# Wk second in each load queue, in a fixed order, a shorter GpSimd chain per z2 tile, 48 warm-up products and a longer order search in a fused attention and gMLP kernel

## The chip, the cores and the metric

The kernel runs on one core of one Trainium2 chip, in one launch. The metric is the device time of that core in microseconds (us). An execution's time is its span in the trace, from the first to the last instruction, plus about 1.75 us. Each execution also records the mean granted clock of TensorE, 1.0 being full speed. Most executions have 0.998 or more, which I call *undisturbed*; some have about 0.993 and are some 2 us longer. The result lists call both kinds "fast" as long as they are within 1.5% of the kernel's fastest run, so the ratios can contain both. Where it matters I also give the undisturbed runs alone. Engine names in the profile: PE is TensorE, PEld its weight load, DVE VectorE, ACT ScalarE, POOL GpSimd, SP SyncE (it issues DMA).

## The reference

Two residual blocks over x of 2048 tokens by 512 (bf16):

```python
x = A_x
h  = x + A(layernorm(x), wqkv, wo)            # linear attention, 32 heads of 16
h2 = h + B(layernorm(h), w_in, w_sp, b_sp, w_out)

# A: q, k, v = split(x @ wqkv); pq, pk = phi(q), phi(k)
#    phi(t) = where(t > 0, t + 1, exp(t)) + 1e-6
#    kv = sum over s of pk v;  z = sum over s of pk;  o = (pq kv) / (pq z + 1e-6);  o @ wo
# B: z = gelu(x @ w_in)               # 2048 x 1792
#    z1, z2 = halves of z;  z2 = layernorm(z2)
#    g = w_sp @ z2 + b_sp             # w_sp is 2048 x 2048, it mixes tokens
#    (z1 * g) @ w_out
```

So there is one barrier: no product with w_sp can finish before the last of the 16 normalized z2 tiles (128 tokens each) is there.

Names in the profile: xn and hn are the normalized x and h, xnT and hnT their transposes; pk is phi(k), pqT is phi(q) transposed, e an exponential on the way to them; st and rs hold statistics and 1/sqrt(variance + epsilon); ident is the identity matrix with which TensorE transposes.

## The kernel before

The kernel records its operations in a list with their data dependences, then a search looks for an order of them with a cost model on the host, and the order that it finds is emitted as five static instruction streams with semaphores. The search is random but seeded, so a source always gives the same streams; any edit of a cost or of an operation gives others.

```python
LOOK = 100.0
ROUNDS = 400
# ... in schedule():
        best = self._swing([-o.prio for o in ops], 20)
        rng = np.random.default_rng(0)
        for _ in range(ROUNDS):
            # ... perturb the starts of a stretch of operations, schedule again
            if got[0] <= best[0]:
                best = got
        self.est, self.start = best
        self.seq = sorted(ops, key=lambda o: (self.start[o.i], o.i))
```

The head: loads, statistics and normalization of x on VectorE and GpSimd, transposes on TensorE, then the wk product:

```python
    load_x("SP", 0, 1, 2000)
    load_x("ACT", 1, 1, 2200)
    load_x("SP", 2, 1, 2700)
    load_x("ACT", 3, 1, 2900)
    for eng, c in (("SP", 0), ("ACT", 2)):
        dma(eng, wqkv[:, c:c + 2, D:2 * D], wq[:, c:c + 2, D:2 * D], f"wk{c}", issue=500, lat=3600, bias=prio())
    load_x("SP", 4, 2, 4600)
    load_x("ACT", 6, 2, 4800)
    # ... x8 to x14, wq
    def rstd(s, r, n, w, col, neg):
        rr, ss = r[:, n:n + w, :], s[:, n:n + w, :]
        pool(lambda p: p.tensor_scalar(rr[:, :, 1:2], ss[:, :, col + 1:col + 2], EPS_LN, None, op0=ALU.add),
             [ss[:, :, col + 1:col + 2]], [rr], 167)
        pool(lambda p: p.tensor_tensor(rr[:, :, 0:1], rr[:, :, 1:2],
                                       expo[:, 0:w].rearrange("p (a b) -> p a b", b=1), ALU.pow), [rr, expo], [rr], 535)
    # ...
    warmup(56)
```

The built order of the loads was x0, x4, x2, wk0, x8 and so on in SP's queue and x1, x3, wk2, x6 in ACT's. A z2 tile takes its moments either from VectorE (the odd tiles and tile 14) or, for the seven other even ones, from the sums that ScalarE accumulates; then GpSimd does six tiny steps:

```python
        if n % 2 == 0 and n < NT - 2:
            gl = act(z2[:, n, :], src, ACT.Gelu_apprx_tanh, FH, accum=s[:, 0:1])
            act(sq_t, z2[:, n, :], ACT.Square, FH, accum=s[:, 1:2])
            pool(lambda p, s=s: p.tensor_scalar(s[:, 12:13], s[:, 0:1], 1.0 / FH, None, op0=ALU.mult), [s], [s], 167)
            pool(lambda p, s=s: p.tensor_scalar(s[:, 1:2], s[:, 1:2], 1.0 / FH, None, op0=ALU.mult), [s], [s], 167)
            pool(lambda p, s=s: p.tensor_tensor(s[:, 2:3], s[:, 12:13], s[:, 12:13], ALU.mult), [s], [s], 167)
            pool(lambda p, s=s: p.tensor_tensor(s[:, 13:14], s[:, 1:2], s[:, 2:3], ALU.subtract), [s], [s], 167)
        else:
            # ... gelu, then bn_stats and bn_aggr on VectorE
        gl.deps.add(table.i)
        rstd(st3, rs3, n, 1, 12, False)
        norm("DVE", z2[:, n, :], z2[:, n, :], st3, rs3, n, 12, FH)
```

Of the kernel before, what the change touches and what calls it, by code (L numbers as in the profile page):

```python
# [6 lines left out]
ACT = mybir.ActivationFunctionType  # L7
ALU = mybir.AluOpType

P = 128  # L10
GRAN = 16
SEM_NS = 45.0
LOOK = 100.0
ROUNDS = 400


class _Op:
    __slots__ = ("i", "eng", "fn", "deps", "cost", "lat", "dma", "prio", "bias", "users",
                 "signal", "count", "clock", "sem", "tag")

    def __init__(self, i, eng, fn, cost, lat, dma, bias):
        self.i, self.eng, self.fn, self.cost, self.lat, self.dma, self.bias = i, eng, fn, cost, lat, dma, bias
        self.deps = set()
        self.users = []
        self.signal = False
        self.count = 0
        self.clock = None
        self.sem = None


class _Prog:
# [93 lines left out]
        return op  # L125

    def _lag(self, p, u):
        return p.lat + (0.0 if p.eng == u.eng == "PE" and p.dma is None else SEM_NS)

    def _pass(self, rank, back):  # L130

        ops = self.ops
        pre = [o.users if back else o.deps for o in ops]
        nxt = [o.deps if back else o.users for o in ops]
        left = [len(p) for p in pre]
        ready = [0.0] * len(ops)
        free = {e: 0.0 for e in self.ENGS}
        cand = {e: [] for e in self.ENGS}
        for o in ops:
            if not left[o.i]:  # L140
                cand[o.eng].append(o.i)
        start = [0.0] * len(ops)
        for _ in ops:
            best = None
            for e in self.ENGS:
                c = cand[e]
                if not c:
                    continue
                t0 = max(free[e], min(ready[i] for i in c))
                pick = min((i for i in c if ready[i] <= t0 + LOOK), key=lambda i: (rank[i], i))  # L150
                t0 = max(t0, ready[pick])
                if best is None or t0 < best[0]:
                    best = (t0, e, pick)
            t0, e, i = best
            cand[e].remove(i)
            start[i] = t0
            free[e] = t0 + ops[i].cost
            for u in nxt[i]:
                lag = self._lag(ops[u], ops[i]) if back else self._lag(ops[i], ops[u])
                ready[u] = max(ready[u], free[e] + lag)  # L160
                left[u] -= 1
                if not left[u]:
                    cand[ops[u].eng].append(u)
        return start
# [23 lines left out]
    def schedule(self):  # L188
        ops = self.ops
        for o in ops:  # L190
            for d in o.deps:
                ops[d].users.append(o.i)
        for o in reversed(ops):
            o.prio = max((ops[u].prio + self._lag(o, ops[u]) for u in o.users), default=o.lat) + o.cost + o.bias
# [3 lines that stand above are left out]
            t = np.array(best[1])  # L198
            a, w = rng.uniform(0, 0.6 * best[0]), rng.uniform(5e3, 4e4)
            if rng.random() < 0.4:  # L200
                a, w = 0.0, best[0]
            near = (t >= a) & (t < a + w)
            got = self._swing(list(t + near * rng.normal(0, rng.choice([200, 600, 1500, 3000]), len(ops))), 2)
# [4 lines that stand above are left out]
        self.order = {e: [o for o in self.seq if o.eng == e] for e in self.ENGS}  # L208
# [91 lines left out]
def bass_sequential_preLN__linear_attn_block__mixer_gmlp__prompt_kernel(  # L300
# [160 lines left out]
    def dma(eng, out_ap, in_ap, name, issue=100.0, lat=2500.0, **k):  # L461
        return g.add(eng, lambda q: q.dma_start(out_ap, in_ap), [in_ap], [out_ap], cost=issue, lat=lat, dma=name, **k)
# [19 lines left out]
                                   base=DH, channel_multiplier=-1), [bmask], [bmask], 350, bias=1e5)  # L482


    later = [1e6]

    def prio():
        later[0] -= 1e3
        return later[0]

    wq = A_wqkv.rearrange("(c p) f -> p c f", p=P)

    def load_w(eng, j, nm, lat):
        dma(eng, wqkv[:, :, j * D:(j + 1) * D], wq[:, :, j * D:(j + 1) * D], nm, issue=500, lat=lat, bias=prio())

    def load_x(eng, n, w, lat):
        dma(eng, x[:, n:n + w, :], x_d[n * P:(n + w) * P, :].rearrange("(n p) d -> p n d", p=P), f"x{n}", issue=500,
            lat=lat, bias=prio())

    def load(eng, dst, src, nm, lat, **k):  # L500
        return dma(eng, dst, src.rearrange("(c p) f -> p c f", p=P), nm, lat=lat, **k)

    load_x("SP", 0, 1, 2000)
    load_x("ACT", 1, 1, 2200)
    load_x("SP", 2, 1, 2700)
    load_x("ACT", 3, 1, 2900)
    for eng, c in (("SP", 0), ("ACT", 2)):
        dma(eng, wqkv[:, c:c + 2, D:2 * D], wq[:, c:c + 2, D:2 * D], f"wk{c}", issue=500, lat=3600, bias=prio())
    load_x("SP", 4, 2, 4600)
    load_x("ACT", 6, 2, 4800)  # L510
    for n, t in ((8, 5100), (10, 5600), (12, 6100), (14, 6700)):
        load_x("SP", n, 2, t)
    load_w("SP", 0, "wq", 7500)
    preload = g.add("ACT", lambda ac: ac.preload_act_table_set("natural_log_exp_and_others"), [], [], cost=1300)


    def stats(src, k, n):
# [1 line left out]
        dve(lambda v: v.bn_stats(s[:, 0:6], src[:, n, :]), [src[:, n, :]], [s[:, 0:6]], D)  # L519
        dve(lambda v: v.bn_aggr(s[:, 6:8], s[:, 0:6]), [s[:, 0:6]], [s[:, 6:8]], 14)  # L520

    def rstd(s, r, n, w, col, neg):

        rr, ss = r[:, n:n + w, :], s[:, n:n + w, :]
        pool(lambda p: p.tensor_scalar(rr[:, :, 1:2], ss[:, :, col + 1:col + 2], EPS_LN, None, op0=ALU.add),  # L525
             [ss[:, :, col + 1:col + 2]], [rr], 167)
        pool(lambda p: p.tensor_tensor(rr[:, :, 0:1], rr[:, :, 1:2],  # L527
                                       expo[:, 0:w].rearrange("p (a b) -> p a b", b=1), ALU.pow), [rr, expo], [rr], 535)
        if neg:
            for i in range(n, n + w):  # L530
                pool(lambda p, i=i: p.tensor_scalar(r[:, i, 2:3], s[:, i, col:col + 1], r[:, i, 0:1], -1.0,
                                                    op0=ALU.mult, op1=ALU.mult), [r[:, i, :], s[:, i, :]], [r[:, i, :]], 167)

    def norm(eng, dst, src, s, r, n, col, w):
        mean, rst, nmr = s[:, n, col:col + 1], r[:, n, 0:1], r[:, n, 2:3]
# [36 lines left out]
            return inst  # L572
        PE(fn, [warm], [bank(7, P)], 2200 + n * 54, bias=1e6)

    warmup(56)

    PAIRS = [0, 2]
    pc = [0]
# [149 lines left out]
    for n in range(NT):  # L728
        b = next_pair()

        def fn(pe, n=n, b=b):
            inst = None
            for c in range(KD):
                pe.matmul(bank(b), lhsT=hnT[:, c, n * P:(n + 1) * P], rhs=win[:, c, FH:FH + GW],  # L734
                          start=c == 0, stop=c == KD - 1)
            for c in range(KD):
                inst = pe.matmul(bank(b + 1, F2), lhsT=hnT[:, c, n * P:(n + 1) * P], rhs=win[:, c, FH + GW:F],  # L737
                                 start=c == 0, stop=c == KD - 1)
            return inst
        PE(fn, [hnT[:, :, n * P:(n + 1) * P], win[:, :, FH:F]], [bank(b), bank(b + 1)], KD * (216 + 162.5))  # L740
        src = pair(b).rearrange("p a b -> p (a b)")[:, 0:FH]
        s = st3[:, n, :]
        if n % 2 == 0 and n < NT - 2:
            gl = act(z2[:, n, :], src, ACT.Gelu_apprx_tanh, FH, accum=s[:, 0:1])
            act(sq_t, z2[:, n, :], ACT.Square, FH, accum=s[:, 1:2])
            pool(lambda p, s=s: p.tensor_scalar(s[:, 12:13], s[:, 0:1], 1.0 / FH, None, op0=ALU.mult), [s], [s], 167)
            pool(lambda p, s=s: p.tensor_scalar(s[:, 1:2], s[:, 1:2], 1.0 / FH, None, op0=ALU.mult), [s], [s], 167)
            pool(lambda p, s=s: p.tensor_tensor(s[:, 2:3], s[:, 12:13], s[:, 12:13], ALU.mult), [s], [s], 167)
            pool(lambda p, s=s: p.tensor_tensor(s[:, 13:14], s[:, 1:2], s[:, 2:3], ALU.subtract), [s], [s], 167)
        else:  # L750
            gl = act(z2[:, n, :], src, ACT.Gelu_apprx_tanh, FH)
            dve(lambda v, n=n, s=s: v.bn_stats(s[:, 0:6], z2[:, n, 0:GW]), [z2[:, n, 0:GW]], [s[:, 0:6]], GW)  # L752
            dve(lambda v, n=n, s=s: v.bn_stats(s[:, 6:12], z2[:, n, GW:FH]), [z2[:, n, GW:FH]], [s[:, 6:12]], F2)
            dve(lambda v, s=s: v.bn_aggr(s[:, 12:14], s[:, 0:12]), [s[:, 0:12]], [s[:, 12:14]], 14)
        gl.deps.add(table.i)
        rstd(st3, rs3, n, 1, 12, False)
        norm("DVE", z2[:, n, :], z2[:, n, :], st3, rs3, n, 12, FH)

    dma("SP", bsp, B_b_sp.partition_broadcast(P), "bsp", issue=1500, lat=2500).deps.add(g.last.i)
# [3 lines left out]
    k = 0  # L763
# [68 lines left out]
```

## Time and profile before

| what | before |
|---|---|
| time | 250.01 us, median of 3 (249.61 to 250.08) |
| span of the profiled run | 248.0 us, clock 1.000 |
| TensorE busy | 240.6 us, of which 56 warm-up products 5.58 |
| TensorE idle after 240 us | 3.10 us |

The page's first part gives the busy time of each engine, its share of the span, and its instructions:

```profile
PE 240.6 (97%) x1196; PEld 111.9 (45%) x1196; DVE 133.1 (54%) x270; ACT 86.2 (35%) x122; POOL 44.6 (18%) x134
```

TensorE is the limit: only its idle time, or time spent on warm-up, can be won. Where it idles shows in the windows view of before. Its columns are the stretch in us, its length, the busy time of PE, PEld, DVE, ACT and POOL with instruction counts, the granted clock, the DMA share and GB/s:

```profile
0.00:10.00 10.00, 7.72 (x77) 6.82 (x78) 6.19 (x17) 2.73 (x4) 4.66 (x22) 1.00 0.82 257
10.00:20.00 10.00, 10.00 (x53) 4.39 (x50) 9.73 (x26) 8.31 (x14) 5.05 (x13) 1.00 0.38 99
20.00:30.00 10.00, 9.55 (x45) 4.33 (x45) 6.84 (x12) 7.29 (x10) 3.02 (x8) 1.00 0.46 92
50.00:70.00 20.00, 19.75 (x91) 8.16 (x90) 19.51 (x34) 18.43 (x20) 2.38 (x6) 1.00 0.49 100
...
95.00:120.00 25.00, 23.70 (x116) 10.68 (x115) 13.73 (x31) 14.54 (x25) 12.75 (x38) 1.00 0.54 115
```

The stretches 30 to 50, 70 to 95 and 120 to 240 us are full. The list of TensorE's waits in before (total us, times, longest) names who ended each gap:

```profile
PE psum L432 <- ACT xnT L451: 0.9, 1, 0.9
PE psum L432 <- DVE z L537: 0.8, 1, 0.8
PE psum L734 <- DMA hnT<-hn: 0.5, 1, 0.5
PE psum L432 <- DVE pk L564: 0.5, 1, 0.5
```

The first is the gap before the first wk product, in the head; here is TensorE's timeline of before there (start us, us, what, and in brackets the idle time before it and what ended it):

```profile
1.22 5.58 PE L571 MATMUL psum<-warm 128*128 128x128 bf16 x56 [1.22 <-POOL warm L469]
6.93 0.72 PE L551 MATMUL psum<-ident,xn 128*128 128x128 bf16 x8
8.58 1.02 PE L432 MATMUL psum<-wqkv,xnT 128*128 128x512 bf16 x4 [0.93 <-ACT xnT L451]
```

The second is the gap of 0.84 us before the first w_sp product at 113.41. The chain of work that ended last shows what led to it. In the stretch from 89 to 114 us of before (start us, us, what) it runs on GpSimd for nearly all the time from 91.8 us on:

```profile
105.64 0.51 POOL st L746
106.22 0.22 POOL st L747
106.51 0.20 POOL st L748
106.78 0.20 POOL st L749
107.06 0.22 POOL rs L525
107.36 0.58 POOL rs L527
107.96 0.51 DVE z L537
```

The six POOL lines from 105.64 on are one even z2 tile: the scaling of two sums, a square, a subtraction, then the addition of epsilon and the power of -1/2. GpSimd's groups of instructions in before, by form (output and input shapes, count, busy us and mean ns, idle before):

```profile
L527 POOL TENSOR_TENSOR rs<-rs,expo 128x1 f32<-128x1 f32 x34 | 20.0, 600 | 1.3
L525 POOL TENSOR_SCALAR rs<-st 128x1 f32<-128x1 f32 x34 | 7.7, 234 | 53.3 <-DVE st L520 49.6 <-DVE st L754 2.9
L746 POOL TENSOR_SCALAR st<-st 128x1 f32<-128x1 f32 x7 | 2.0, 288 | 3.2 <-ACT sq L451 2.7
L749 POOL TENSOR_TENSOR st<-st 128x1 f32<-128x1 f32 x7 | 1.6, 227 | 0.5
L747 POOL TENSOR_SCALAR st<-st 128x1 f32<-128x1 f32 x7 | 1.5, 218 | 0.3
L748 POOL TENSOR_TENSOR st<-st 128x1 f32<-128x1 f32 x7 | 1.5, 209 | 0.5
```

One number in each of 128 partitions costs 0.2 to 0.3 us here, and the power 0.6 us.

### The profile page before, as it was taken

How to read it: one execution, taken by the hardware profiler on the slowest of the kernel's cores; microseconds unless marked ns; L12 is line 12 of the kernel's file. 1: busy time of each engine (PE TensorE's matmuls, PEld its weight loads, DVE VectorE, ACT ScalarE, POOL GpSimd, SP SyncE). 2: the span in 40 equal slices, each digit the busy share in tenths (PEclk: the TensorE clock that was granted, in tenths of full speed). 3: DMA queues.
4: the chain of work that ended last, by engine and by line, in shares of the span. 5: the costliest groups of instructions: out<-in, count | busy, mean ns of one | idle time of the engine just before them, and what ended most of it. 6: DMA issues, size and time to landing. Idle time of an engine off the chain costs nothing.

```text
span 248.0 us, 3139 instructions
## 1 busy us (share of the span) xinstructions
PE 240.6 (97%) x1196; PEld 111.9 (45%) x1196; DVE 133.1 (54%) x270; ACT 86.2 (35%) x122; POOL 44.6 (18%) x134
## 2 busy tenths in 40 slices
PE   8899999999999999998999999999999999999994
PEld 8443444534444454543444444444444444444441
DVE  3998565689999998482233322332123201443064
ACT  2588533699985679861000000000021000010020
POOL 5356000001125889751000000000000000000000
PEclk9999999999999999999999999999999999999999
DMA  6925396444544555554444542000000000102022
GB/s 194 313 46 107 83 382 218 102 105 90 94 100 102 106 87 100 151 115 85 106 101 96 89 100 62 0 0 3 0 0 0 3 0 0 63 24 74 11 71 99
DMA packets 57198, 21.57 MB, mean 87 GB/s; under 512 B 49504, under 2 KB 56544, under 8 KB 57184
## 3 DMA queue, kind: packets, MB, share of 16 engines
q1 hardware_dynamic: 56352, 20.59, 34.0%
q10 hardware_dynamic: 832, 0.79, 1.0%
q8 instruction: 9, 0.15, 0.2%
q14 instruction: 5, 0.04, 0.1%
HBM read 7.47 MB, written 2.10 MB: 39 GB/s over the span
## 4 chain that ended last, share of the span: by engine, by line
PE 65%; DVE 18%; POOL 8%; ACT 4%; issue 2%; DMA 2%; SPq 0%; POOLq 0%
PE psum L432 60%; POOL rs L527 5%; DVE st L519 5%; PE psum L613 4%; DVE h L715 4%; POOL rs L525 2%; ACT r L451 2%; DMA x<-in_A_x_dram 2%; DVE pqT L704 1%; DVE pk L564 1%; ACT e L451 1%; DVE z L537 1%; DVE pqT L564 1%; DVE hn L537 1%; DVE st L752 1%
## 5 line engine op out<-in xcount | busy, mean ns | idle before, releaser
L432 PE MATMUL psum<-wsp,z 128*128 128x512 bf16 x448 | 97.7, 379 | 0.8 <-DVE z L537 0.8
L432 PEld LDWEIGHTS psum<-wsp,z 128*128 128x128 bf16 x448 | 43.7, 98 | 54.0 <-DVE z L537 1.3
L451 ACT ACTIVATE z1T<-psum 128x512 bf16<-128x512 f32 x28 | 16.6, 596 | 121.4 <-PE psum L432 121.4
L795 DVE TENSOR_TENSOR u<-psum,bsp 128x512 bf16<-128x512 f32 x28 | 19.4, 691 | 53.6 <-PE psum L432 53.4
L797 DVE TENSOR_TENSOR z1T<-u,z1T 128x512 bf16<-128x512 bf16 x28 | 11.9, 424 | 29.1 <-ACT z1T L451 28.6
L432 PE MATMUL psum<-hnT,win 128*128 128x512 bf16 x112 | 26.5, 379 | 0.0
L432 PE MATMUL psum<-wout,z1T 128*128 128x512 bf16 x112 | 25.7, 379 | 0.0
L527 POOL TENSOR_TENSOR rs<-rs,expo 128x1 f32<-128x1 f32 (+1 forms) x41 | 25.1, 621 | 1.8
L451 ACT ACTIVATE e<-psum 128x1024 bf16<-128x1024 f32 (+1 forms) x18 | 16.6, 923 | 12.8 <-PE psum L432 12.3
L525 POOL TENSOR_SCALAR rs<-st 128x1 f32<-128x1 f32 (+1 forms) x41 | 9.3, 233 | 60.5 <-DVE st L520 56.7
L451 ACT ACTIVATE z<-psum 128x896 bf16<-128x896 f32 x16 | 14.6, 914 | 7.5 <-PE psum L737 7.2
L432 PE MATMUL psum<-wqkv,xnT 128*128 128x512 bf16 x64 | 15.7, 379 | 1.4 <-ACT xnT L451 0.9
L432 PEld LDWEIGHTS psum<-wout,z1T 128*128 128x128 bf16 x112 | 10.9, 98 | 13.4 <-DVE ost L785 0.6
L734 PE MATMUL psum<-win,hnT 128*128 128x512 bf16 x64 | 16.4, 379 | 0.5 <-DMA hnT<-hn 0.5
L613 PE MATMUL psum<-pk,xn 128*128 128x512 bf16 x64 | 16.4, 379 | 0.0
L432 PEld LDWEIGHTS psum<-hnT,win 128*128 128x128 bf16 x112 | 10.2, 98 | 13.4 <-ACT z1T L451 2.8
L432 PE MATMUL psum<-xnT,wqkv 128*128 128x512 bf16 x64 | 15.8, 379 | 0.3 <-DVE pqT L564 0.3
L432 PE MATMUL psum<-m,pqT 128*128 128x512 bf16 x64 | 15.7, 380 | 0.0
L785 DVE TENSOR_TENSOR ost<-psum,h 128x512 bf16<-128x512 f32 x16 | 10.4, 686 | 8.7 <-PE psum L432 8.6
L737 PE MATMUL psum<-win,hnT 128*128 128x384 bf16 x64 | 13.0, 326 | 0.0
L519 DVE BATCH_NORM_STATS2 st<-x 128x6 f32<-128x512 bf16 x16 | 10.4, 677 | 3.8 <-DMA x<-in_A_x_dram 3.8
L563 DVE TENSOR_SCALAR e<-e 128x1024 bf16<-128x1024 bf16 (+1 forms) x18 | 7.1, 394 | 9.4 <-ACT e L451 9.2
(67 smaller groups left out, 204.8 us busy)
## 6 DMA issues: line engine op xcount, KB each, us to landing
out_dram<-ost SPq DMA_DIRECT2D x16, 128.0 KB, 1.7
win<-in_B_w_in_dram SPq DMA_DIRECT2D x1, 1792.0 KB, 8.2
x<-in_A_x_dram SPq DMA_DIRECT2D x5, 256.0 KB, 7.0
wqkv<-in_A_wqkv_dram SPq DMA_DIRECT2D x2, 512.0 KB, 8.7
wsp<-in_B_w_sp_dram SPq DMA_TRANSPOSE x64, 2.9
wout<-in_B_w_out_dram SPq DMA_DIRECT2D x1, 896.0 KB, 11.1
wo<-in_A_wo_dram SPq DMA_DIRECT2D x1, 512.0 KB, 3.4
bsp<-in_B_b_sp_dram SPq DMA_DIRECT2D x1, 512.0 KB, 4.4
```

The source lines that it names most:

```text
L432: inst = pe.matmul(out_ap, lhsT=a, rhs=b, start=start and i == 0, stop=stop and i == len(pairs) - 1)
L451: return g.add("ACT", lambda ac: ac.activation(out_ap, in_ap, func, **kw), [in_ap, *extra], [out_ap] + ([accum] if accum is not None else []),
L519: dve(lambda v: v.bn_stats(s[:, 0:6], src[:, n, :]), [src[:, n, :]], [s[:, 0:6]], D)
L525: pool(lambda p: p.tensor_scalar(rr[:, :, 1:2], ss[:, :, col + 1:col + 2], EPS_LN, None, op0=ALU.add), [ss[:, :, col + 1:col + 2]], [rr], 167)
L527: pool(lambda p: p.tensor_tensor(rr[:, :, 0:1], rr[:, :, 1:2], expo[:, 0:w].rearrange("p (a b) -> p a b", b=1), ALU.pow), [rr, expo], [rr] ...
L613: inst = pe.matmul(bank(CB[c]), lhsT=xn[:, i, c * P:(c + 1) * P], rhs=pk[:, i, :], start=i == 0, stop=i == NT - 1)
L715: dve(lambda v, n=n, b=b: v.tensor_tensor(h[:, n, :], bank(b), x[:, n, :], ALU.add), [bank(b), x[:, n, :]], [h[:, n, :]], D, ps=True)
L734: pe.matmul(bank(b), lhsT=hnT[:, c, n * P:(n + 1) * P], rhs=win[:, c, FH:FH + GW], start=c == 0, stop=c == KD - 1)
L737: inst = pe.matmul(bank(b + 1, F2), lhsT=hnT[:, c, n * P:(n + 1) * P], rhs=win[:, c, FH + GW:F], start=c == 0, stop=c == KD - 1)
L785: dve(lambda v: v.tensor_tensor(o, bank(b), h[:, n, :], ALU.add), [bank(b), h[:, n, :]], [o], D, ps=True)
L795: dve(lambda v, t=t, b=b, tok=tok: v.tensor_tensor(t, bank(b), bsp[:, tok], ALU.add), [bank(b), bsp[:, tok]], [t], GW, ps=True)
L797: dve(lambda v, t=t, z=z: v.tensor_tensor(z, t, z, ALU.mult), [t, z], [z], GW, acc=2)
```

## The change

It does four things at once. It fixes the order of the loads in each queue (through "soft" predecessors that order the issue without a wait) with wk second and gives the search's cost model later landing times and longer GpSimd steps; the aim is an earlier first wk product. It takes three GpSimd steps out of an even z2 tile: ScalarE's Square gets a scale, so that its sum is the mean of squares, VectorE forms mean² minus that (the negative variance), and the addition of epsilon multiplies by -1. It lets the search look further (160 instead of 100) and longer (1200 rounds instead of 400). It takes 8 warm-up products away.

```diff
-LOOK = 100.0
-ROUNDS = 400
+LOOK = 160.0
+ROUNDS = 1200
# ... soft predecessors in the search, cut
-    load_x("SP", 0, 1, 2000)
-    load_x("ACT", 1, 1, 2200)
-    load_x("SP", 2, 1, 2700)
-    load_x("ACT", 3, 1, 2900)
+    load_x("SP", 0, 1, 2650)
+    load_x("ACT", 1, 1, 2850)
     for eng, c in (("SP", 0), ("ACT", 2)):
-        dma(eng, wqkv[:, c:c + 2, D:2 * D], wq[:, c:c + 2, D:2 * D], f"wk{c}", issue=500, lat=3600, bias=prio())
-    load_x("SP", 4, 2, 4600)
-    load_x("ACT", 6, 2, 4800)
+        first_load(eng, wqkv[:, c:c + 2, D:2 * D], A_wqkv[c * P:(c + 2) * P, D:2 * D], f"wk{c}", 4800)
+    load_x("SP", 2, 1, 5300)
+    load_x("ACT", 3, 1, 5300)
+    load_x("SP", 4, 2, 6800)
+    load_x("ACT", 6, 2, 6800)
# ... later loads, and new costs of the GpSimd steps for the search, cut
-        pool(lambda p: p.tensor_scalar(rr[:, :, 1:2], ss[:, :, col + 1:col + 2], EPS_LN, None, op0=ALU.add),
-             [ss[:, :, col + 1:col + 2]], [rr], 167)
+        pool(lambda p: p.tensor_scalar(rr[:, :, 1:2], ss[:, :, col + 1:col + 2], sign, EPS_LN, op0=ALU.mult,
+                                       op1=ALU.add), [ss[:, :, col + 1:col + 2]], [rr], 230)
-    warmup(56)
+    warmup(48)
-            act(sq_t, z2[:, n, :], ACT.Square, FH, accum=s[:, 1:2])
+            act(sq_t, z2[:, n, :], ACT.Square, FH, scale=FH ** -0.5, accum=s[:, 1:2])
             pool(... mean ...)
-            pool(... E2 / FH ...)
-            pool(... mean * mean ...)
-            pool(... E2 - mean^2 ...)
+            dve(lambda v, s=s: v.scalar_tensor_tensor(s[:, 13:14], s[:, 12:13], s[:, 12:13], s[:, 1:2], op0=ALU.mult,
+                                                      op1=ALU.subtract), [s], [s], 60)
+            rstd(st3, rs3, n, 1, 12, False, -1.0)
```

(The lines with dots shorten the GpSimd steps shown above.)

More of the change, by code (lines that the diff above doesn't have):

```diff
@@ L12 @@
 SEM_NS = 45.0
-LOOK = 100.0
-ROUNDS = 400
+LOOK = 160.0
+ROUNDS = 1200
 class _Op:
     __slots__ = ("i", "eng", "fn", "deps", "cost", "lat", "dma", "prio", "bias", "users",
-                 "signal", "count", "clock", "sem", "tag")
+                 "signal", "count", "clock", "tag", "soft")
     def __init__(self, i, eng, fn, cost, lat, dma, bias):
@@ L27, in __init__ @@
         self.clock = None
-        self.sem = None
+        self.soft = set()
 class _Prog:
@@ L127, in _lag @@
     def _lag(self, p, u):
+        if p.i in u.soft:
+            return 0.0
         return p.lat + (0.0 if p.eng == u.eng == "PE" and p.dma is None else SEM_NS)
@@ L132, in _pass @@
         ops = self.ops
-        pre = [o.users if back else o.deps for o in ops]
-        nxt = [o.deps if back else o.users for o in ops]
+        pre = [o.users if back else o.deps | o.soft for o in ops]
+        nxt = [o.deps | o.soft if back else o.users for o in ops]
         left = [len(p) for p in pre]
@@ L190, in schedule @@
         for o in ops:
-            for d in o.deps:
+            for d in o.deps | o.soft:
                 ops[d].users.append(o.i)
@@ L482, in bass_sequential_preLN__linear_attn_block__mixer_gmlp__prompt_kernel @@
                                    base=DH, channel_multiplier=-1), [bmask], [bmask], 350, bias=1e5)
-    later = [1e6]
-    def prio():
-        later[0] -= 1e3
-        return later[0]
     wq = A_wqkv.rearrange("(c p) f -> p c f", p=P)
-    def load_w(eng, j, nm, lat):
-        dma(eng, wqkv[:, :, j * D:(j + 1) * D], wq[:, :, j * D:(j + 1) * D], nm, issue=500, lat=lat, bias=prio())
-    def load_x(eng, n, w, lat):
-        dma(eng, x[:, n:n + w, :], x_d[n * P:(n + w) * P, :].rearrange("(n p) d -> p n d", p=P), f"x{n}", issue=500,
-            lat=lat, bias=prio())
@@ L500, in load @@
-    def load(eng, dst, src, nm, lat, **k):
-        return dma(eng, dst, src.rearrange("(c p) f -> p c f", p=P), nm, lat=lat, **k)
-    load_x("SP", 0, 1, 2000)
-    load_x("ACT", 1, 1, 2200)
-    load_x("SP", 2, 1, 2700)
-    load_x("ACT", 3, 1, 2900)
-    for eng, c in (("SP", 0), ("ACT", 2)):
-        dma(eng, wqkv[:, c:c + 2, D:2 * D], wq[:, c:c + 2, D:2 * D], f"wk{c}", issue=500, lat=3600, bias=prio())
-    load_x("SP", 4, 2, 4600)
-    load_x("ACT", 6, 2, 4800)
-    for n, t in ((8, 5100), (10, 5600), (12, 6100), (14, 6700)):
+    queue = {"SP": [], "ACT": []}
@@ new lines, in load, with first_load, load_x @@
+    def load(eng, dst, src, nm, lat, issue=500.0):
+        return dma(eng, dst, src.rearrange("(c p) f -> p c f", p=P), nm, lat=lat, issue=issue)
+    def first_load(eng, dst, src, nm, at):
+        q = queue[eng]
+        op = load(eng, dst, src, nm, at - 500.0 * (len(q) + 1))
+        op.bias = 1e6
+        if q:
+            op.soft.add(q[-1].i)
+        q.append(op)
+    def load_x(eng, n, w, at):
+        first_load(eng, x[:, n:n + w, :], x_d[n * P:(n + w) * P, :], f"x{n}", at)
+    load_x("SP", 0, 1, 2650)
@@ L512, in bass_sequential_preLN__linear_attn_block__mixer_gmlp__prompt_kernel @@
+    load_x("ACT", 1, 1, 2850)
+    for eng, c in (("SP", 0), ("ACT", 2)):
+        first_load(eng, wqkv[:, c:c + 2, D:2 * D], A_wqkv[c * P:(c + 2) * P, D:2 * D], f"wk{c}", 4800)
[3 more added lines that the diff above has]
+    load_x("ACT", 6, 2, 6800)
+    for n, t in ((8, 7600), (10, 8300), (12, 9100), (14, 9900)):
         load_x("SP", n, 2, t)
-    load_w("SP", 0, "wq", 7500)
-    preload = g.add("ACT", lambda ac: ac.preload_act_table_set("natural_log_exp_and_others"), [], [], cost=1300)
+    first_load("SP", wqkv[:, :, 0:D], A_wqkv[:, 0:D], "wq", 11400)
@@ L517, in stats @@
+    g.add("ACT", lambda ac: ac.preload_act_table_set("natural_log_exp_and_others"), [], [], cost=1300).soft.add(
+        queue["ACT"][-1].i)
     def stats(src, k, n):
@@ L520, in stats, with rstd @@
         dve(lambda v: v.bn_aggr(s[:, 6:8], s[:, 0:6]), [s[:, 0:6]], [s[:, 6:8]], 14)
-    def rstd(s, r, n, w, col, neg):
+    def rstd(s, r, n, w, col, neg, sign=1.0):
         rr, ss = r[:, n:n + w, :], s[:, n:n + w, :]
-        pool(lambda p: p.tensor_scalar(rr[:, :, 1:2], ss[:, :, col + 1:col + 2], EPS_LN, None, op0=ALU.add),
-             [ss[:, :, col + 1:col + 2]], [rr], 167)
+        pool(lambda p: p.tensor_scalar(rr[:, :, 1:2], ss[:, :, col + 1:col + 2], sign, EPS_LN, op0=ALU.mult,
+                                       op1=ALU.add), [ss[:, :, col + 1:col + 2]], [rr], 230)
         pool(lambda p: p.tensor_tensor(rr[:, :, 0:1], rr[:, :, 1:2],
-                                       expo[:, 0:w].rearrange("p (a b) -> p a b", b=1), ALU.pow), [rr, expo], [rr], 535)
+                                       expo[:, 0:w].rearrange("p (a b) -> p a b", b=1), ALU.pow), [rr, expo], [rr],
+             620 + 120 * (w - 1))
         if neg:
@@ L531, in rstd @@
                 pool(lambda p, i=i: p.tensor_scalar(r[:, i, 2:3], s[:, i, col:col + 1], r[:, i, 0:1], -1.0,
-                                                    op0=ALU.mult, op1=ALU.mult), [r[:, i, :], s[:, i, :]], [r[:, i, :]], 167)
+                                                    op0=ALU.mult, op1=ALU.mult), [r[:, i, :], s[:, i, :]], [r[:, i, :]], 240)
     def norm(eng, dst, src, s, r, n, col, w):
@@ L744, in bass_sequential_preLN__linear_attn_block__mixer_gmlp__prompt_kernel @@
             gl = act(z2[:, n, :], src, ACT.Gelu_apprx_tanh, FH, accum=s[:, 0:1])
-            act(sq_t, z2[:, n, :], ACT.Square, FH, accum=s[:, 1:2])
-            pool(lambda p, s=s: p.tensor_scalar(s[:, 12:13], s[:, 0:1], 1.0 / FH, None, op0=ALU.mult), [s], [s], 167)
-            pool(lambda p, s=s: p.tensor_scalar(s[:, 1:2], s[:, 1:2], 1.0 / FH, None, op0=ALU.mult), [s], [s], 167)
-            pool(lambda p, s=s: p.tensor_tensor(s[:, 2:3], s[:, 12:13], s[:, 12:13], ALU.mult), [s], [s], 167)
-            pool(lambda p, s=s: p.tensor_tensor(s[:, 13:14], s[:, 1:2], s[:, 2:3], ALU.subtract), [s], [s], 167)
+            act(sq_t, z2[:, n, :], ACT.Square, FH, scale=FH ** -0.5, accum=s[:, 1:2])
+            pool(lambda p, s=s: p.tensor_scalar(s[:, 12:13], s[:, 0:1], 1.0 / FH, None, op0=ALU.mult), [s], [s], 190)
+            dve(lambda v, s=s: v.scalar_tensor_tensor(s[:, 13:14], s[:, 12:13], s[:, 12:13], s[:, 1:2], op0=ALU.mult,
+                                                      op1=ALU.subtract), [s], [s], 60)
+            rstd(st3, rs3, n, 1, 12, False, -1.0)
         else:
@@ L754, in bass_sequential_preLN__linear_attn_block__mixer_gmlp__prompt_kernel @@
             dve(lambda v, s=s: v.bn_aggr(s[:, 12:14], s[:, 0:12]), [s[:, 0:12]], [s[:, 12:14]], 14)
+            rstd(st3, rs3, n, 1, 12, False)
         gl.deps.add(table.i)
-        rstd(st3, rs3, n, 1, 12, False)
         norm("DVE", z2[:, n, :], z2[:, n, :], st3, rs3, n, 12, FH)
```

## The prediction

> **What bounds the kernel now.** TensorE. The page's busy table gives it 240.6 us of a 248.0 us span (97%), VectorE 54%, GpSimd 18%. The timeline shows 128x512 products at 216 ns each once it streams (608 in 131.5 us). So only time in which TensorE does nothing useful can be won. Its timeline and waits list it: real work begins at 6.93 us (after 56 warm-up products, 1.22 to 6.80); 0.93 us before the first wk product at 8.58; 0.45 at 20.1 (a pk from VectorE); 0.26 at 55.3; 0.46 at 98.3 (a transposed hn tile); 0.84 at 112.6 (the last z2 tile from VectorE); and 3 us of tail after the last product. Gaps inside: about 2.9 us, nearly all that is to be had.
>
> **GpSimd and z2.** From 91.8 to 107.9 us the chain of waits runs mostly through GpSimd. An even z2 tile costs six steps there: 288, 218, 209, 227, 234 and 600 ns (groups by form). The change keeps the mean (288), the add (234, now with a multiply) and the power (600), and gives one tiny step to VectorE (an estimate, from the aggregate steps: 0.1 to 0.15 us). Saved: 209+218+227 = 0.65 us plus gaps of 0.08 each, 0.9 us a tile, some 6 us over seven tiles. VectorE then finishes the last z2 tile 1.5 to 2 us earlier. The same 24 products still lie between the last z2 products and the first w_sp product (built order), so the 0.84 gap closes, and most of the 0.46 one, as the hn tiles share GpSimd. Worth 1.0 to 1.4 us.
>
> **Head.** Loads of both queues share the same engines: the Trainium skill, "DMA: Bandwidth & Descriptors", section "Issuing engines are not separate DMA queues"; the trace agrees, its windows show about 250 to 380 GB/s in total from 3 to 10 us whichever queue issues. With wk second in each queue it should land near 5.7 us instead of 7 to 8.5; the first product should start near 7.2 instead of 8.58. Eight fewer warm-up products free TensorE 0.5 us earlier. But x2 and x3 now land behind wk, at 6.1 to 6.8, and the built order puts the statistics of x3 before the normalization of tile 1 on VectorE, and those of x6 and x4 before that of tile 2. VectorE is busy almost without a break from 10 to 20 us and sets TensorE's pace there (the 0.45 gap), so what it loses early it doesn't win back. I expect VectorE 0 to 1 us later: the early first product is mostly idle time moved. Net head: -0.3 to +0.8 us, middle +0.3.
>
> **Rest.** The longer search reorders z1 and w_out products; TensorE streams there already: 0 to -0.3. The tail stays 3 us.
>
> Sum: -1.2 +0.3 -0.2 = -1.1 us: **248.9 us**, range 247.0 to 250.5. Faster by over 2%: 0.03. Within 2%: 0.95. Slower by over 2%: 0.02.
>
> **What would show it.** Right: first wk product before 7.6 us; VectorE waiting 0.5 us or more for x3 or x6; TensorE gaps of 0.3 us or more between 8 and 20 us; GpSimd busy about 39 us; no gap before the first w_sp product. Wrong: VectorE waits for no load after x0 and the head ends a microsecond earlier.
>
> **What would make it wrong.** Landings earlier than I read (then 247 to 248); a clock that stays low after the shorter warm-up, making early products twice as long (251); a new wait where the search moved work late.

## The result, and the profile after

| | before | after |
|---|---|---|
| time, median of 6 runs each | 249.75 us (249.13 to 250.08) | 249.19 us (248.48 to 249.49) |
| ratio of the fast runs | | 0.9978, 95% interval 0.9958 to 0.9998 |
| span of the profiled run | 248.0 us | 247.5 us |

A ratio is the mean time of one kernel's fast runs over that of the other's of the same rounds, so it is not quite the ratio of the medians quoted. The change saves about half a microsecond, 0.2%; all runs of after were undisturbed.

Busy time of after, from the page; VectorE has 2.3 us more, 1.4 of it its seven new steps (207 ns each), GpSimd 3.9 us less:

```profile
PE 239.2 (97%) x1188; PEld 110.7 (45%) x1188; DVE 135.4 (55%) x277; ACT 86.4 (35%) x122; POOL 40.7 (16%) x113
```

The same windows of after:

```profile
0.00:10.00 10.00, 6.63 (x64) 5.18 (x64) 5.48 (x14) 3.27 (x5) 4.23 (x20) 1.00 0.84 267
10.00:20.00 10.00, 9.45 (x55) 4.46 (x56) 9.81 (x26) 7.58 (x12) 4.08 (x10) 1.00 0.29 76
20.00:30.00 10.00, 9.90 (x47) 4.34 (x46) 8.03 (x17) 7.90 (x10) 4.27 (x12) 1.00 0.45 93
50.00:70.00 20.00, 18.88 (x86) 7.69 (x85) 19.35 (x34) 19.36 (x21) 3.55 (x6) 1.00 0.49 96
...
95.00:120.00 25.00, 24.81 (x123) 11.45 (x121) 14.90 (x38) 16.70 (x30) 12.97 (x33) 1.00 0.54 112
```

Three things happened. *First*, up to 30 us TensorE was busy for 27.27 us before and 25.98 after. Without the warm-up (5.58 and 4.29 us) that is 21.69 us of work in both: between these two profiles the head gained nothing. (It varies from profile to profile: after's order again gave 21.59 us, before's order with 48 warm-up products 22.52, in a run in which VectorE waited for no load after x0.) *Second*, from 95 to 120 us it did 24.81 - 23.70 = 1.11 us more. *Third*, from 50 to 70 us it did 19.75 - 18.88 = 0.87 us less. The idle time after 240 us fell from 3.10 to 2.97. The sum -1.11 + 0.87 - 0.13 leaves -0.37; the rest of the 0.5 us of the spans (-0.13) is that TensorE's busy time without warm-up came out 0.13 us shorter (235.04 and 234.91), about what modelled ends leave uncertain.

TensorE's waits in after:

```profile
PE psum L555 <- DVE xn L541: 2.1, 3, 1.4
PE psum L738 <- DMA hnT<-hn: 0.6, 2, 0.4
PE psum L434 <- DVE h L719: 0.4, 1, 0.4
PE psum L434 <- DVE pqT L708: 0.2, 1, 0.2
```

The wait for z is gone, and the chain of after in the same stretch, 89 to 114 us, has no GpSimd work in it. It waits for one transposed hn tile, and from 98.67 us TensorE follows on itself:

```profile
95.17 3.37 DMA hnT<-hn
98.53 0.14 issue
98.67 1.02 PE psum L738 x4
```

In GpSimd's groups of after, L750 is the mean, L528 the multiply and add, L530 the power; the lines of the three other steps are gone:

```profile
L530 POOL TENSOR_TENSOR rs<-rs,expo 128x1 f32<-128x1 f32 x34 | 19.5, 578 | 2.3
L528 POOL TENSOR_SCALAR rs<-st 128x1 f32<-128x1 f32 x34 | 8.5, 250 | 54.6 <-DVE st L523 49.5 <-DVE st L758 3.2 <-DVE st L751 0.5
L750 POOL TENSOR_SCALAR st<-st 128x1 f32<-128x1 f32 x7 | 1.7, 247 | 3.0 <-ACT sq L453 2.6
```

The head of after, on TensorE's timeline:

```profile
1.77 4.29 PE L575 MATMUL psum<-warm 128*128 128x128 bf16 x48 [1.77 <-POOL warm L471]
5.89 0.39 PE L555 MATMUL psum<-ident,xn 128*128 128x128 bf16 x4
7.64 0.40 PE L555 MATMUL psum<-ident,xn 128*128 128x128 bf16 x4 [1.36 <-DVE xn L541]
7.87 1.89 PE L434 MATMUL psum<-wqkv,xnT 128*128 128x512 bf16 x8
10.03 0.40 PE L555 MATMUL psum<-ident,xn 128*128 128x128 bf16 x4 [0.27 <-DVE xn L541]
10.95 0.40 PE L555 MATMUL psum<-ident,xn 128*128 128x128 bf16 x4 [0.52 <-DVE xn L541]
```

The wk products start 0.71 us earlier (7.87 against 8.58), but idle time stands on both sides of them: TensorE waits 1.36, 0.27 and 0.52 us for normalized x tiles. VectorE had waited 0.80 us, until 6.57, for the load of x3, whose statistics come in its order ahead of the normalization of tile 1. The warm-up began 0.55 us later and ended 0.74 us earlier (6.06 against 6.80), and that time too was spent waiting.

### The profile page after: what moved, and what is told of

The parts are those of the page before. It is cut to its first block, busy times and chain, and to the rows that moved or that the text cites. A ratio compares the mean times of both kernels' runs of the same rounds, so it can differ in the third digit from the quotient of the medians.

```text
span 247.5 us, 3104 instructions
## 1 busy us (share of the span) xinstructions
PE 239.2 (97%) x1188; PEld 110.7 (45%) x1188; DVE 135.4 (55%) x277; ACT 86.4 (35%) x122; POOL 40.7 (16%) x113
## 4 chain that ended last, share of the span: by engine, by line
PE 68%; DVE 17%; DMA 5%; ACT 4%; POOL 2%; issue 2%; ACTq 0%
PE psum L434 61%; DVE st L522 4%; DVE h L719 3%; PE psum L617 3%; DMA hnT<-hn 3%; PE psum L738 2%; DMA x<-in_A_x_dram 2%; DVE hn L541 2%; PE psum L741 2%; POOL rs L530 1%; ACT r L453 1%; DVE pk L568 1%; ACT xn L453 1%; DVE st L756 1%; ACT e L453 1%
## 5 line engine op out<-in xcount | busy, mean ns | idle before, releaser
L530 POOL TENSOR_TENSOR rs<-rs,expo 128x1 f32<-128x1 f32 (+1 forms) x41 | 24.4, 600 | 2.9
L528 POOL TENSOR_SCALAR rs<-st 128x1 f32<-128x1 f32 (+1 forms) x41 | 9.9, 242 | 64.6 <-DVE st L523 59.4
```

## The experiments

**The theory** (T): the z2 steps alone give what was gained, about 1 us; the load order gives nothing because VectorE, not wk, paces the head; the new order of the search opened the gaps at 50 to 70 us. **Rivals**: (R1) the gain comes from the search, and z2 alone gives nothing; (R2) the load order gains in the head and the search's order there gives it away; (R3) the shorter warm-up costs or gains on its own.

To change one part without reshuffling everything, I replaced the search in most experiments by its own result, a table of operation numbers:

```diff
-        best = self._swing([-o.prio for o in ops], 20)
-        # ... ROUNDS random trials, cut
-        self.seq = sorted(ops, key=lambda o: (self.start[o.i], o.i))
+        self.seq = [ops[i] for i in ORDER]      # before's (or after's) order, frozen
```

With the table unchanged this gives the same stream on every engine as the search does. All kernels were correct. They ran in three jobs (the second on the chip of the first, the third on another), each beside 11 runs of before: medians 249.48, 250.21 and 249.68 us, undisturbed ones 249.47, 250.03 and 249.62.

### z2_alone: before's order, with the change's z2 steps

The diff is the z2 part and the `rstd` part of the change; in the table the new VectorE step stands where the removed ones stood.

> The kernel before, its found order of instructions frozen, with only the z2 steps of the change (GpSimd three steps for an even tile where there were six, one small VectorE step more). Theory (GpSimd's chain holds the last z2 tile and some hn tiles): 0.8 to 1.3 us faster than before, TensorE's gap before the first w_sp product (0.84 us before) gone, GpSimd busy about 39 us, the 50 to 70 us stretch as before (TensorE busy 19.75 of 20). Rival (VectorE is the engine that is short from 50 to 95 us, so seven more steps there, which wait in order for GpSimd, give it back): 0 to 0.4 us of gain, new waits of VectorE on GpSimd.

Measured: median 249.17 us, ratio 0.9995 (0.9951 to 1.004). That mixes two kinds of runs: four undisturbed ones (248.42, 248.55, 248.67, 249.68; median 248.61) and two of 251.15 and 251.19 at clock 0.993 and 0.991. Undisturbed against undisturbed, it is 0.86 us faster than before (249.47). The profile fell on a disturbed run, in which x2 landed late. TensorE's timeline of it, and the first line of its windows view, in which the clock stands at 0.92 in the place of before's 1.00:

```profile
8.63 1.03 PE L584 MATMUL psum<-ident,xn 128*128 128x128 bf16 x8 [2.29 <-DVE xn L570]
```

```profile
0.00:10.00 10.00, 6.22 (x65) 5.79 (x66) 4.52 (x12) 2.01 (x3) 4.07 (x20) 0.92 0.78 242
```

TensorE waited 2.29 us, and toward the end of that wait the clock was halved, from 8.48 to 11.89 us (the trace's clock record). That loses at most half of 3.41 us, 1.7 us, on top of the wait. So this run was 2.21 us late at the products pk by ones (the sum of pk over the tokens, a landmark for kernels of the same order; 46.15 against 43.94 us in before), yet only 1.41 us late at the first w_sp product (114.82 against 113.41): 0.80 us was regained between, there was no wait before that product, and GpSimd's busy time was 39.4. That is not the late head letting GpSimd catch up: loads_alone, below, has the same order and the old steps, was 1.28 us late at the products pk by ones (45.22) and 1.27 at the first w_sp product (114.68), and still waited 0.86 us before it. The gap for a transposed hn tile did not close in z2_alone: 0.63 us, where before had 0.46. From 50 to 70 us TensorE was busy 19.75 us, as in before. This supports T for z2 and is against R1.

### loads_alone: before's order, with the change's load order

```diff
# issue order in each queue, all other streams as in before
-SP:  x0 x4 x2 wk0 x8 x10 x12 wq x14
-ACT: x1 x3 wk2 x6
+SP:  x0 wk0 x2 x4 x8 x10 x12 x14 wq
+ACT: x1 wk2 x3 x6
```

> The kernel before with its order frozen, only the order of the input loads is that of the change (wk second on each queue). Theory (VectorE paces the head and waits for x3 and x2 in its order): VectorE stands 0.7 us or more for x3 before it normalizes tile 0, which moves from 6.47 to about 7.7 us; first wk product at about 9 us; 0.3 to 1.0 us slower than before. Rival (the late wk held the head): first wk product before 8 us, 0.3 to 0.6 us faster.

Measured: median 251.34 us, ratio 1.0072 (1.0032 to 1.0113). Three undisturbed runs had 250.22, 250.98 and 251.05, three more 251.63 to 253.39 at clock 0.993. It lost more than expected: 1.5 us undisturbed (250.98 against 249.47). VectorE's timeline shows the cause, and TensorE's below it what came of it:

```profile
6.95 1.29 DVE L552 BATCH_NORM_STATS2 st<-x 128x6 f32<-128x512 bf16 x2 [1.95 <-DMA x<-in_A_x_dram]
```

```profile
8.61 0.72 PE L584 MATMUL psum<-ident,xn 128*128 128x128 bf16 x8 [2.63 <-DVE xn L570]
9.70 1.04 PE L465 MATMUL psum<-wqkv,xnT 128*128 128x512 bf16 x4 [0.37 <-ACT xnT L484]
```

With wk ahead of x2 and x3, and VectorE still asking for the statistics of a later tile before it normalizes tile 0, the first wk product came at 9.70 us, later than in before (8.58). So R2's first half fails: the load order alone gains nothing. With the order that the search made for it, in after, it costs nothing either.

### warm_alone: before's order, 48 warm-up products

```diff
-    warmup(56)
+    warmup(48)
```

> The kernel before with its order frozen and 48 warm-up products in place of 56. Theory (VectorE's tile 0 is what the first transposes wait for, at 6.8 us): within 0.2 us of before, the first transposes still at 6.8 to 6.95 us, warm-up ending at about 6.0 to 6.3. Rival (the clock is granted late without the eight products): products of 128x512 at 430 ns for some of the first, 0.5 us or more slower.

Measured: 249.30, 249.38, 249.60 and 251.47 us undisturbed, one run of 251.80 at clock 0.993 and one slow. In the profiled run (249.30) the warm-up ended at 6.53 us, the first transposes began at 6.65 and the first wk product at 7.76, at full speed (1.04 us for four products); VectorE waited for no load after x0. The late clock of the rival isn't seen. Three of four undisturbed runs equal before; the 251.47 is unexplained. I count the warm-up as worth 0. Whether fewer warm-up products make a disturbed head more frequent is not settled: 2 of 6 runs here had a reduced clock, 5 of before's 33 had.

### search_alone: LOOK 160 and ROUNDS 1200, nothing else

```diff
-LOOK = 100.0
-ROUNDS = 400
+LOOK = 160.0
+ROUNDS = 1200
```

> The kernel before with only the scheduler's two settings of the change (look-ahead 160, 1200 rounds), searched anew. Theory (the search's estimate of a schedule doesn't see what costs half a microsecond on the chip, so a longer search gives another draw and no gain): between 0.8 us faster and 0.8 us slower, gaps of TensorE between 50 and 70 us differing from before's 0.25 us by 0.3 us or more in either direction. Rival (the longer search is where the change's gain comes from): 0.5 us or more faster, by fewer gaps between 90 and 115 us.

Measured: 250.67 us (250.47 to 251.10, 5 runs, all undisturbed), ratio 1.0042 (1.001 to 1.0073): 1.2 us slower. TensorE was busy 25.00 us of the stretch 95 to 120, so its order closed the w_sp gap with the six old steps; but from 10 to 20 us it was busy 9.26 us instead of 10.00 and from 50 to 70 us 19.07 instead of 19.75. The line of the windows view for 50 to 70 us, to set beside before's:

```profile
50.00:70.00 20.00, 19.07 (x88) 7.88 (x87) 19.39 (x33) 18.29 (x20) 1.96 (x4) 1.00 0.48 95
```

The search keeps an order only if its cost model puts it no later; what it found here is slower on the chip. So a new order alone, without the z2 steps or the loads, can open gaps at 50 to 70 us: the three kernels above, with before's order throughout, have 19.75, 19.74 and 19.60 us there. But before's order in that stretch is not enough to avoid them: head_after_rest_before, head_mix and z2_head_split, below, have it there after other heads, and 19.13, 19.29 and 19.09 us of work. And a new order can also close the w_sp gap without the z2 steps. The new costs that the whole change gives the search were not tried alone.

### head_after_rest_before: after's head, before's order for the rest

```diff
# order table over after's operations
-ORDER = after's order throughout
+ORDER = after's order up to its first q product, before's order from there on
```

> The changed kernel with its operations, loads and 48 warm-up products, its own found order up to the first q product (about 23.8 us), and the order of the kernel before from there on. Theory (the gain of the z2 steps, about 0.9 us in the undisturbed runs of z2_alone, was given back at 50 to 70 us, where the new search left 1.1 us of gaps against 0.25): 0.5 to 0.9 us faster than the changed kernel, so about 248.3 to 248.7 where before takes 249.4; TensorE busy 19.6 us or more of 20 between 50 and 70 us, and no gap before the first w_sp product. Rival (VectorE, busy without a break from 50 to 95 us, forces about 1 us of TensorE gaps whatever the order): the gaps show up elsewhere before 113 us and the time stays at that of the changed kernel.

Measured: 251.24 us (250.65 to 252.33), ratio 1.0036 (0.999 to 1.0081). The expectation failed. The seam of the two orders made a wait of 0.9 us for a pk tile, and 50 to 70 us had 19.13. Here the cut made new waits; the run does not say what after's head is worth, and it does not exclude the rival.

### norm1_first: after, with tile 1 normalized before the statistics of x3

```diff
-    ..., 30, 31, 33, 32, 51, 34, 36, 35, 49, ...
+    ..., 30, 31, 33, 32, 36, 51, 34, 35, 49, ...      # 36 normalizes tile 1, 51 is the statistics of x3
```

> The changed kernel with its order frozen and one swap on VectorE: tile 1 is normalized before the statistics of x3, not after them. Theory (VectorE's own work sets the head's pace; the swap uses 0.3 us of the 0.8 us it stands waiting for x3): first transposes of tile 1 about 0.8 us earlier (from 7.64), yet only 0.1 to 0.4 us faster than the changed kernel. Rival (TensorE's 1.36 us gap before those transposes is itself on the path): 0.7 us or more faster.

Measured: 248.97 us (248.69 to 249.55), ratio 0.9941 (0.9901 to 0.998). The eight transposes now ran together from 6.87 us, but the products pk by ones began at 43.12 us, in after at 43.19: the earlier start was given back before 43 us. The ratio looks better than after's mostly since three of before's 11 runs in this job had a reduced clock; with undisturbed runs alone it is 0.9964. It was repeated, below.

### head_mix: x3 before wk in one queue

```diff
# on the kernel of head_after_rest_before; order of VectorE's early statistics fitted to it
-ACT: x1 wk2 x3 x6
+ACT: x1 x3 wk2 x6
```

> As head_after_rest_before, with the head rearranged: x3 goes ahead of wk on its queue, VectorE does the statistics of x3 before it normalizes tile 0 and those of x2 before tile 1, and the statistics of x6 and x7 come after tiles 2 and 3 are normalized. Theory (VectorE paces the head; it now has no wait for a load after x0): VectorE idle under 0.4 us between 3.5 and 20 us, tile 3 normalized about 1 us earlier than in the changed kernel (9.58 us there), 0.4 to 1.0 us faster than head_after_rest_before, about 247.5 to 248.2. Rival (the loads or ScalarE pace it): wk lands after 7.5 us or x4 late, no gain.

Measured: 251.11 us (250.82 to 251.31), ratio 1.0023 (0.9984 to 1.0062), so no gain over its base. VectorE no longer waited for x3, but one load further on:

```profile
8.98 1.29 DVE L554 BATCH_NORM_STATS2 st<-x 128x6 f32<-128x512 bf16 x2 [1.81 <-DMA x<-in_A_x_dram]
```

The wait moved from x3 to x4. In every head with wk ahead of x2 and x3, or of one of them, VectorE waited for a load after x0: between 0.23 us (norm1_first) and 1.95 (loads_alone), 0.80 in after and 1.81 here (in before 0.31). Whichever load goes first, another comes later. That fits what the Trainium skill, "DMA: Bandwidth & Descriptors", section "Issuing engines are not separate DMA queues", says of loads from several engines: they end on the same DMA engines and interleave. The traces do not separate the two queues, but the total is the same whatever the order: in the first 10 us the mean DMA share was 0.82 in before, 0.84 in after and 0.82 in loads_alone, at 257 to 267 GB/s.

### after_seed2: after with another seed of the search

```diff
-        rng = np.random.default_rng(0)
+        rng = np.random.default_rng(2)
```

> The changed kernel with only the start value of the search's random numbers changed. Theory (where the gaps between 50 and 115 us fall is the luck of the search's draw, not a property of the change): a time 0.4 us or more away from the changed kernel in either direction, with gaps in other places. Rival (the change itself fixes the time): within 0.3 us, and the 1.1 us of gaps again between 50 and 70 us.

Measured: 249.96 us (249.84 to 250.67), ratio 0.9984 (0.9944 to 1.0024). The gaps are elsewhere: 7.88 us of work from 10 to 20 us, 19.90 from 50 to 70, 24.16 from 70 to 95, 25.00 from 95 to 120. So the 0.87 us at 50 to 70 us is not forced by the change. It is the luck of one order, and another seed has gaps at other places, and more of them.

### after_again: after with its own order frozen

> The changed kernel once more, its found order frozen (the same instructions on every engine), so that the others of this call can be compared with it on one chip. Expected 0.1 to 0.4% faster than before; if before again shows runs at a granted clock of 0.993 and this kernel none, the changed head also keeps the clock, which the medians hide.

Measured: 249.18 us (248.71 to 249.68, all undisturbed), ratio 0.9967 (0.9935 to 1.0). This repeats the result in another job: 0.50 us under before's median, where the first had 0.56. In this profile 50 to 70 us had 18.25 us of work, so the gaps there come back. The gap for a transposed hn tile at 99 us is back too: 0.44 us. For the longest gap at 50 to 70 us, 0.78 us before the product at 69.54 with a transposed hn tile, SP's timeline names a likely cause. VectorE had normalized that tile by 64.90 us, but in SP's order its transposing DMA stands behind three transposing loads of w_sp:

```profile
61.85 5.11 SPq L499 DMA_TRANSPOSE wsp<-in_B_w_sp_dram  x3
67.00 1.27 SPq L499 DMA_TRANSPOSE hnT<-hn  x1
```

So the tile lay ready for 2.1 us. In after it was ready at 65.00 and its transposing began at 65.89, and the gap was 0.42 us. No run moved these loads.

### norm1_first_again: the repeat

> norm1_first again, beside the changed kernel on the same chip. Theory (VectorE paces the head): 0.1 to 0.4 us faster than after_again, as the swap earns VectorE 0.3 us. Rival (TensorE's gap before the transposes of tile 1 is on the path): 0.7 us or more faster. No difference: the swap's time is waited off further on.

Measured: six undisturbed runs with median 249.46, one of 251.43 at clock 0.993; ratio 0.9966 (0.9931 to 1.0001). No gain over after_again on the same chip: the first result for norm1_first did not hold.

### after_old_z2: after's order, with the old six z2 steps

The diff is the z2 part of the change backwards, with the three old steps where the VectorE step stood.

> The changed kernel with its order frozen and only the z2 steps of the kernel before put back (six steps on GpSimd for an even tile). Theory (the shorter GpSimd chain is what the change gains): 0.6 to 1.5 us slower than after_again, with TensorE waiting for a z2 or an hn tile between 90 and 115 us and GpSimd busy 45 us. Rival (the new order hides GpSimd, and the gain comes from loads or order): within 0.3 us.

Measured: 252.66 us (251.20 to 254.18), ratio 1.01 (1.0056 to 1.0145); undisturbed 251.20, 251.22, 252.18 and 253.13. In after's order, two undisturbed runs lost 2.0 us to after_again's median of 249.18 and two 3 to 4 us. The list of TensorE's waits names it:

```profile
PE psum L467 <- DVE z L574: 2.6, 1, 2.6
```

GpSimd was busy 45.6 us again, and the first w_sp product came at 117.21 us, in after_again at 114.31. In this profile the clock was also lost, from 118.10 to 121.52 us, after that wait: again 1.7 us. It is more than I expected; my reading, not tested, is that the order was found for short chains and leaves no room for long ones.

### z2_head_split: z2_alone with x4 and x5 loaded apart and the head fitted to it

```diff
-    load_x("SP", 4, 2, 4600)
+    load_x("SP", 4, 1, 4600)
+    load_x("ACT", 5, 1, 4600)
-    warmup(56)
+    warmup(52)
# and before's order table with wk third in each queue, the tiles 0 and 1 normalized before the statistics of x4
```

> z2_alone (order of the kernel before, new z2 steps) with a head fitted to the loads: both tiles x2 and x3 ahead of wk, x4 and x5 as single tiles on the two queues after it, tile 0 and tile 1 normalized as soon as GpSimd allows, the wk product of tile 1 ahead of the transposes of tiles 2 and 3, 52 warm-up products. Theory: first wk product near 7.5 us where before has 8.58, VectorE without a wait of over 0.6 us for a load after x0, no run at a granted clock of 0.993; 1.0 to 1.6 us faster than before in undisturbed runs (0.3 to 0.8 better than z2_alone). Rival (the sum of bytes paces the head): VectorE waits a microsecond or more for x4 or x5, no better than z2_alone.

Measured: 249.89 us (249.59 to 250.58, all undisturbed), ratio 0.9999 (0.9968 to 1.0031). The first wk product came at 7.57 us as intended, and it bought nothing: VectorE waited 0.81 us for the next load, a wait of 0.9 us for a transposed hn tile came at 99 us, and 50 to 70 us had 19.09. It is 1.3 us slower than z2_alone's four undisturbed runs on the other chip.

### Which is best

No version clearly beats after. z2_alone has the lowest undisturbed median (248.61, four runs, ratio to undisturbed before 0.9966 by the medians), but a third of its runs had a reduced clock, and its ratio with all runs is 0.9995. There is a pattern in the counts. With before's loads (before in the three jobs, z2_alone, warm_alone, search_alone) 9 of 50 runs had a reduced clock; with the change's loads and an order made for them (after, after_again, norm1_first and its repeat, head_after_rest_before, after_seed2) 1 of 37. I left out loads_alone (3 of 6) and after_old_z2 (2 of 6; its profiled run lost the clock only after the wait for z2). So part of what the changed head is worth may be fewer disturbed runs. Only the profiled ones show where the clock was lost, so this is an observation and not a shown cause.

## Why the prediction was right or wrong

The outcome was right: 249.19 us lies within 247.0 to 250.5, near 248.9, and in the class "within 2%". The gain against the runs of before in the same rounds was 0.56 us, where 1.1 was predicted. The hit says little by itself: the range is 3.5 us wide and holds before's 249.75 as well. That the time came within 0.3 us of 248.9 is partly luck, since the 1.1 us were taken off a before of 250.01 and before had 249.75 in these rounds. Point by point:

1. *TensorE bounds it, and only the gaps and the tail can be won.* Right; the whole result is a shift of gaps of 0.1 to 1.4 us.
2. *The z2 steps: "worth 1.0 to 1.4 us".* Right: 1.11 us more work from 95 to 120 us; the gap before the first w_sp product closed, and the one for hn at 98 us fell from 0.46 to 0.19 (but in after_again it was 0.44, and in z2_alone 0.63: that part of the claim is not shown). Alone, in before's order, the steps gave 0.86 us undisturbed, and put back into after's order the old ones cost at least 2 us. In another order they were not needed: search_alone had 25.00 us of work there with six steps. GpSimd came to 40.7, not "about 39". The multiply-and-add took 250 ns where the add had taken 234, on 34 instructions. VectorE's new step took 207 ns, the estimate having been 0.1 to 0.15 us from aggregate steps; it is no bottleneck. One such step was no faster on VectorE than on GpSimd (209 to 227 ns for the three that went): the gain is that one took the place of three, and on another engine.
3. *Head: "-0.3 to +0.8 us, middle +0.3".* Right, at 0.0. VectorE waited 0.80 us for x3 and TensorE had gaps of 0.27 and 0.52 us at 10 and 10.95 us, as predicted. The sign "first wk product before 7.6 us" failed by 0.3: the built order puts the transposes of tile 1 ahead of it, and these waited for VectorE until 7.64. The claim "idle time moved" is what the runs show: norm1_first and z2_head_split both brought early work forward and gained nothing by it.
4. *"Rest: the longer search reorders z1 and w_out products; TensorE streams there already: 0 to -0.3".* **This is the step that failed.** The order changed everywhere, and from 50 to 70 us TensorE did 0.87 us less: its gaps came to 1.12 us where before had 0.25, among them 0.18 us for a pqT tile, 0.40 for h and 0.42 for a transposed hn tile. There VectorE is busy 19.35 and ScalarE 19.36 of 20 us, which leaves little slack (before: 19.51 and 18.43). search_alone shows that a new order alone can open gaps there; the kernels with before's order throughout have at most 0.40 us, but those with before's order after another head have 0.71 to 0.91. So the gaps depend on the order and on the head before it. Why each one arises is shown for none; for the hn tile the likely place is SP's order (after_again). The prediction named "a new wait where the search moved work late" as a risk, and gave it no term in the sum. With +0.87 in place of -0.2 its sum would be about zero; the head and the tail being a little better than its middle values give the rest.
5. *Tail: stays 3 us.* Right: 2.97.

The parts do not add. Undisturbed against before, z2 gave -0.9, the warm-up 0, the loads +1.5 and the search +1.2: together +1.8 us, where the whole change gave -0.5. The load order costs only in an order not made for it, and the new search has to be judged with the operations that it ordered. Removing the z2 part from the whole, on the other hand, cost at least 2 us where adding it alone had gained 0.9. Each of these numbers holds only in its own order. What stays open: which of VectorE, ScalarE or SP's order of the hn transposes sets the pace from 50 to 70 us, and the influence of the warm-up count on disturbed runs.

## What to carry to other kernels

When a search or a scheduler lays out the program, an edit comes with a new order, and the new order alone made this kernel 1.2 us slower, more than the edit was worth; so freeze the order to measure an edit, and try seeds and orders on the chip afterwards. Shorten the chain of small steps that ends last before a barrier; that gain was real, but it is capped by the gap that was there (0.84 and 0.46 us), however much busy time (3.9 us) leaves the engine. In a head where all loads share the same bandwidth, moving one load forward moves another back: look for the engine that consumes them in order. Look also at the order in a DMA queue later on: a small transfer that TensorE waits for may stand behind loads that are needed much later, as the hn tile did in after_again.

## What the Trainium skill lacked or had wrong

- "TensorE: Matmul & The Clock Gate", Part 1, gives the cold state as what follows "≥1 idle window (~3.4µs)", and its subsection "HAM oscillation" has the rule "no PE-idle gaps >~3.4µs". The window's length agrees: by the clock records of the traces the halved stretches here were 3.41 us (8.48 to 11.89 us in z2_alone, 118.10 to 121.52 in after_old_z2), and the grants at the start came at times between 4.3 and 7.5 us (the windows view prints 1.00 before the first grant too). I counted windows of 3.41 us on from each grant. But the clock was lost after windows that were not idle: TensorE was busy for 1.28 us of 3.41 in z2_alone and 1.29 in norm1_first_again; it was kept after windows with 1.67 (loads_alone) and 1.76 us (after_seed2). So a single wait of 2.29 us was enough in z2_alone and cost up to 1.7 us more by the halved clock, while one of 2.63 us in loads_alone cost none: it was divided between two windows. The page has no threshold of that kind.
- "GPSIMD Engine Reference", section 3.1, takes a large tensor_tensor apart and gives about 156 ns of dispatch per instruction for VectorE; in GpSimd's column it names the parts of the dispatch without a figure, so what a step on one element per partition costs can't be read from it. Here such steps took 209 to 288 ns and the power 578 to 600 ns (means of the groups), with gaps of about 0.08 us between two steps; a VectorE step on one element per partition took 207 ns.
- "DMA: Bandwidth & Descriptors", section "Issuing engines are not separate DMA queues": the heads measured here fit it. It does not say what the practical consequence was: with a load of 256 KB ahead of one of 128 KB in each of the two queues, VectorE waited 1.95 us for the smaller ones in loads_alone, where it had waited 0.31 us in before.
